# Linear attention with a gated feed-forward: other DRAM rows and transfers for the last 64 rows of x, for w1's last rows and for the folded output weight

## Chip, cores, metric

The kernel runs on one core of one Trainium2 chip. The metric is device microseconds of one execution; lower is better. Before the change three runs took 1108.54, 1109.60 and 1109.98 us (median 1109.6).

## What is computed

x is 2048 x 576, everything in fp32. Two branches read the normalized xn and are multiplied:

```
xn = layernorm(x)
q, k, v = heads(xn @ wqkv)                 # 32 heads of 18
phi(t) = (t + 1 if t > 0 else exp(t)) + 1e-6
kv = sum_s phi(k)_s v_s ;  z = sum_s phi(k)_s
s = concat_heads(phi(q) kv / (phi(q) z + 1e-6)) @ wo
g = silu(gelu(xn @ w1 + b1) @ w2 + b2)     # 4608 hidden units
out = x + s * g
```

## The kernel before, in words

**Precision.** TensorE multiplies in fp32r. Each operand is kept as a high part h (a cast) and a low part l (the rest), and a product is h·h + h·l + l·h: per 128 rows of the contraction three matmuls.

**The contraction of 576** is four blocks of 128 and a last block of 64 rows. These 64 rows ("the rest") are not three matmuls but one: their h and l rows are laid into the 128 partitions, and one matmul against a suitably doubled weight tile gives all terms.

**Stages.** (1) 0 to 157 us: normalize and transpose x, k and v projections, the state kv. (2) 157 to 291 us: the query projection (`query`, line 415), `fold_wo` (line 554), which multiplies kv into wo once so that attention needs one product per tile, and per token tile `transpose_p`, `attend`. (3) from 291 us: the feed-forward, in two halves of nine steps. A step takes four blocks of 128 hidden units: two `Up` objects n (line 963, 14 products in all, 7 matmuls of 512 columns each: six for two blocks of 128 rows, the seventh for the rest), then the down products (`pm`, line 1114). Both matrix products use a seven-product scheme (of Winograd's kind) over 2x2 blocks, so seven different sums of x's blocks are wanted, numbered 1 to 7. An `Up` takes them in the order 1, 6, 7, 5, 2, 3, 4. The first half has one set of x sums, the second half another; between them, in the ninth step, all x tiles are exchanged.

**x sums in DRAM.** `x_dram` holds the 28 blocks for the half that comes later; `X_PARTS` (line 1270) names the seven transfers of 1 MB each (h0, l0, s2, h1, l1, s1, s4), `X_AT` the step at which each is issued. The rests are made apart by the class `Rest` (line 775), for half 0 and half 1 beside stage 2: `gather` collects h and l of the 64 rows, `whole` adds them and sends them through `rr_dram` to shift partitions, `sums` forms the Winograd sums, `split` makes h and l again and stores them in `rq_dram`: two stores of 128 rows for each of two tiles. `load_rest` (line 822) reads one product's rest: two transfers, each of 32 DRAM rows read twice into 64 partitions, 2 KB a row: h into partitions 0 to 63, l into 64 to 127. Rests 1, 6 and 7 go beside their x parts into a free fifth block of h0, s2, h1; rests 5, 2, 3 and 4 into the tile `rxm` (`load_rests`, line 953: eight transfers).

**w1's last rows** lie in `we_dram`. `load_we` (line 678) reads for each n 64 rows of 3584 B, and the same rows again into the other 64 partitions: two transfers.

**fold_wo** computes kv·wo in groups of 126 rows, but the weight is wanted in blocks of 128 rows. The shift is done by DMA from SBUF to SBUF: of group i, the first k = 2i rows go to the end of block i-1 (line 581), the others, 126 - k, to the head of block i (line 584): transfers of 124, 122 and 120 rows. ScalarE (`split_kw`, line 261) casts a block as soon as it is there, then VectorE forms its low part (line 262).

**Order.** All DMAs here are issued by SP, one after the other. Up to the end of stage 2 and in the feed-forward the order of PE, DVE, ACT and POOL is the program's (`in_order`); SP's is chosen by the scheduler from the same program order. In the feed-forward `plans` (line 1322) names at which product a load, cast or sum is issued. DMAs take their completion semaphores from a ring of eight, so a DMA can only be issued when the one eight before it has landed.

Of the kernel before, what the change touches and what calls it, by code (L numbers as in the profile page):

```python
# [8 lines left out]
F32 = mybir.dt.float32  # L9
# [15 lines left out]
KT = 5  # L25
# [17 lines left out]
def linear_attention_gated_ffn(ctx, tc, x, wqkv, wo, w1, w1e, b1, w2, b2, out):  # L43
# [42 lines left out]
    def as2(ap):  # L86
        return ap.rearrange("p (a b) -> p a b", a=2)
# [26 lines left out]


    rr_dram = dram.tile([2, P, 512], F32, name="rr_dram")
    rq_dram = dram.tile([2, 2, P, 2, 512], F32, name="rq_dram")
    we_dram = dram.tile([WG, P, 2, WB * P], F32, name="we_dram")
    c_dram = dram.tile([2, P, QH, 2, HD], F32, name="c_dram")

# [433 lines left out]
    def fold_wo():  # L554

        (kr0, kw1), (kw2, kw3) = (
            (t[:, 0], t[:, 1]) for t in (kw_pair("kw01"), kw_pair("kw23"))
        )
        kw4 = stage(D, "kw4")
        kw = [kr0, kw1, kw2, kw3, kw4]  # L560

        for i, n, at in [(i, G, i * G) for i in range(4)] + [(4, 8, 4 * G), (4, P, 512)]:
            rows = GROUPS[i][1]
            for h in range(2):
                hs = slice(h * HD, (h + 1) * HD)
# [12 lines left out]
            if 0 < i and n < P:  # L578

                k = 2 * i  # L580
                nc.sync.dma_start(krs[-1][P - k :], kw[i][:k])
                if i < 4:
                    krs.append(stage(D, f"kr{i}"))
                    nc.sync.dma_start(krs[-1][: G - k], kw[i][k:G])
            elif i == 0:
                krs.append(kr0)

# [90 lines left out]
    def load_we(n):  # L678

        we_sb[n] = w1p.tile([P, WB, P], F32R, tag="we", name=f"we_{n}", bufs=2)  # L680
        dst = we_sb[n].bitcast(F32).rearrange("p b c -> p (b c)")
        g, q = divmod(n % NP, WG)
        src = we_dram[q, 32 * g : 32 * g + 32].rearrange("r v c -> (r v) c")
        for k in range(2):
            nc.sync.dma_start(dst[64 * k : 64 * k + 64], src)

    WE_AT = {1: 0, 2: 1, 3: 2, 5: 3, 7: 4, 6: 5, 4: 6}

# [83 lines left out]
    nc.gpsimd.memset(sgn[64:96, 1:2], 1.0)  # L772
    nc.gpsimd.memset(sgn[96:, 1:2], -1.0)

    class Rest:
        def __init__(self, half):
            self.half = half
# [1 line left out]

        def two(self, n):  # L780
            t = w1_tile("a", f"rest{self.half}{n}").rearrange("p k c -> p (k c)")
            return t[:, :512], t[:, 512:1024]

        def gather(self):
            self.q, lo = (v.bitcast(F32) for v in self.two("q"))
            for b in range(2):
                rows = slice(64 * b, 64 * b + 64)
                nc.sync.dma_start(self.q[rows], self.b[b][:64, 4].bitcast(F32))
                nc.sync.dma_start(lo[rows], self.b[b][64:, 4].bitcast(F32))
            self.lo = lo  # L790

        def whole(self):
            q, rr = self.q, rr_dram[self.half]
            nc.vector.tensor_tensor(q, q, self.lo, op=ADD)
            nc.sync.dma_start(rr, q)
            self.e, self.f = (v.bitcast(F32) for v in self.two("ef"))
            self.g, self.m = (v.bitcast(F32) for v in self.two("gm"))
            A0, B0, A1, B1 = (rr[32 * k : 32 * k + 32] for k in range(4))
            for k, (e, f) in enumerate(((A0, A1), (A1, B1)) * 2):
                nc.sync.dma_start(self.e[32 * k : 32 * k + 32], e)  # L800
                nc.sync.dma_start(self.f[32 * k : 32 * k + 32], f)
            nc.sync.dma_start(self.g[64:96], B0)
            nc.sync.dma_start(self.g[96:], A0)
            nc.sync.dma_start(self.m[64:96], B1)

        def split(self, k):
            src = (self.q, self.e)[k]
            h, l = t = self.two(f"s{k}")
            nc.scalar.copy(h, src)
            nc.vector.tensor_tensor(l, src, h.bitcast(F32), op=SUB)  # L810
            for v in range(2):
                nc.sync.dma_start(rq_dram[self.half, k, :, v], t[v].bitcast(F32))

        def sums(self):
            e, g, m, up = self.e, self.g, self.m, slice(64, P)
# [1 line left out]
            nc.vector.scalar_tensor_tensor(e[up], g[up], sgn[up, 1:2], e[up], op0=MUL, op1=ADD)  # L817
            nc.vector.tensor_tensor(e[64:96], e[64:96], m[64:96], op=SUB)

    REST_AT = {1: 0, 2: 1, 4: 3, 7: 4, 5: 5, 3: 6, 6: 7}  # L820

    def load_rest(half, i, dst):

        k, at = divmod(REST_AT[i], 4)
        for v in range(2):
            src = rq_dram[half, k, 32 * at : 32 * at + 32, v]
            nc.sync.dma_start(
                dst[64 * v : 64 * v + 64].bitcast(F32),
                bass.AP(tensor=src.tensor, offset=src.offset, ap=[[1024, 32], [0, 2], [1, 512]]),
            )  # L830

    EW1 = nc.gpsimd
    EL1 = nc.vector
# [22 lines left out]
    def beside(i, k):  # L856

        if k == 0:
            if i == 3:
                split_kw(3, nc.vector)  # L860
            if i == 4:
                xsum[0] = XSums(0, tmp_w1)
            if i == 5:
                xsum[1] = XSums(2, lambda name: as2(kw_pair(name).rearrange("p a d -> p (a d)")[:, :1024]))
            sums(i)
            if i in RESTS:
                half, what, *k = RESTS[i]
                if half not in rests:
                    rests[half] = Rest(half)
                getattr(rests[half], what)(*k)  # L870
        else:
            if i == 16:
                sums(i)
            if i == 17:
                z = xsum[1]
                z.split(z.u, z.s3, nc.vector)
            if i in SPLITS:
                half, n = SPLITS[i]
                z = xsum[half]
                if i in (8, 12):  # L880
                    z.place(not half)
                z.split(z.u if n == 3 else z.t, getattr(z, f"s{n}"), nc.vector)
                if not half:
                    spill(i - 8)
            if i == 12:
                w2_raw0.append(load_w2_raw(0))
                w1t[0] = W1(0)
            if i == 13:
                w1t[1] = W1(1)
            if i == 16:  # L890
                load_we(0)
                z = xsum[1]
                load_rest(1, 1, z.h0[:, 4])
                load_rest(1, 6, z.tiles[0][:, 4])
                load_rest(1, 7, z.h1[:, 4])
            if i == 17:
                w = w1t[0]
                w.hi("a"), w.lo("a")
                for j in (5, 6, 7, 4):
                    w.T(j)  # L900
                w.hi(6), w.lo(6)
            if i == 18:
                load_we(1)
                w = w1t[0]
                for j in ("c", "d"):
                    w.hi(j), w.lo(j)
# [44 lines left out]
    rxm = xp.tile([P, KT, 512], F32R, tag="xh1", name="rxm")  # L951

    def load_rests(half):
        out = {}
        for k, i in enumerate((5, 2, 3, 4)):
            out[i] = rxm[:, k]
            load_rest(half, i, out[i])
        return out

    mid = md.tile([P, 5, 512], F32, name="mid")  # L960
    m1_sb, u1_sb, u2_sb = (mid[:, i] for i in range(3))
# [297 lines left out]

    def x_operands(h0, l0, h1, l1, s1, s2, s4, rs):  # L1260
        A, B = slice(0, 2), slice(2, 4)
        rs = {1: h0[:, 4], 6: s2[:, 4], 7: h1[:, 4], **rs}
        return {i: (*v, rs[i]) for i, v in {
            1: (h0[:, A], l0[:, A]), 2: (h0[:, B], l0[:, B]), 4: (h1[:, B], l1[:, B]),
            7: (h1[:, A], l1[:, A]), 5: (s1[:, A], s1[:, B]), 6: (s2[:, A], s2[:, B]),
            3: (s4[:, A], s4[:, B]),
        }.items()}


    X_PARTS = {  # L1270
        "h0": (0, x_hi, 0, 1), "s4": (24, x_lo, 1, None), "l0": (4, x_lo, 2, None),
        "s2": (16, x_hi, 2, 6), "s1": (20, x_lo, 0, None), "h1": (8, x_hi, 3, 7),
        "l1": (12, x_lo, 3, None),
    }
    X_AT = {"h0": 8, "l0": 11, "s2": 11, "h1": 13, "l1": 13, "s1": 13, "s4": 14}
# [2 lines left out]
    def load_x_part(k):  # L1278
# [1 line left out]
        x_new[k] = make_tile(at, f"{k}r")  # L1280
        nc.sync.dma_start(x_new[k][:, :4].bitcast(F32), x_dram[:, a : a + 4])
        if i:
            load_rest(0, i, x_new[k][:, 4])

    UP = (1, 6, 7, 5, 2, 3, 4)
    NS = 28
# [49 lines left out]
    w2t[0].load_raw()  # L1336
    z = xsum[1]
    s2, s1, s4 = z.tiles
    xs = x_operands(z.h0, z.l0, z.h1, z.l1, s1, s2, s4, load_rests(1))
    seq = ExitStack()  # L1340
    seq.enter_context(in_order(nc.vector.engine, nc.scalar.engine, nc.gpsimd.engine, nc.tensor.engine))
    n_chunks = 2 * NC
    for step in range(n_chunks):
# [59 lines left out]
        if half == 1 and c >= 2:  # L1403
            for k in range(2 + 2 * plain):
                tiles = {}
                t, at, done = (6 + c, 0, 4) if k < 2 else (7 + c, 5, 9)
                def load(k=k, t=t, tiles=tiles):
                    tiles[0] = finish_tiles(k)
                    finish_load(t, k % 2, tiles[0])
# [74 lines left out]
```

## Time and profile before

| | us |
|---|---|
| median of three runs | 1109.6 |
| the profiled execution | 1109.0 |
| its span, first to last instruction | 1107.3 |
| outside the span | 1.7 |
| PE busy | 1094.5 |
| DVE busy | 799.7 |
| POOL busy | 454.2 |
| ACT busy | 453.1 |
| granted TensorE clock | 0.999 |

How to read it: an engine's busy time is what its instructions took; PE is TensorE. A row of the chain reads "start, length, what": the chain runs back from the last instruction through whatever released each one. A row of the timeline reads "start, length, engine, line, operation, out<-in", and in brackets how long the engine had been idle and who ended that. In the table by stretches the last two columns are the mean busy share of the 16 DMA engines and the rate at which they moved data. "SPq" is SP issuing a DMA. In names, `a`, `b`, `e`, `zy` are PSUM tiles of an `Up`; `h0r`, `s4r` and so on are the x parts read back for the second half; `wa`, `wc`, `wd` are w1 operands.

### The profile page before, as it was taken

Reading aid. Unit: us, or ns where it says so; the run is one execution under the profiler, and the core shown is the slowest. Engines: PE = TensorE matmul, PEld = TensorE weight load, DVE = VectorE, ACT = ScalarE, POOL = GpSimd, SP = SyncE. Lnnn points to the kernel's source line nnn. Section 1 sums busy time; section 2 is a strip of 40 time slices with the busy share of each in tenths; the row PEclk is TensorE's granted clock in tenths of the full one; section 3 lists DMA queues with packets and bytes.
Section 4 is the critical chain, followed back from the end, with each engine's and each line's share of the span. In section 5 each row is a group of like instructions: output and inputs, shape, how many; then the busy total and the mean of one; then the engine's idle time right before and its main releaser. Section 6 shows DMA issues by size and latency. Waiting matters only on the chain.

```text
span 1107.3 us, 18602 instructions
## 1 busy us (share of the span) xinstructions
PE 1094.5 (99%) x6972; PEld 1018.5 (92%) x6972; DVE 799.7 (72%) x1163; ACT 453.1 (41%) x768; POOL 454.2 (41%) x392
## 2 busy tenths in 40 slices
PE   8999999999999999999999999999999999999998
PEld 8999998999998998989989889799898998988977
DVE  7665447989687787978878878667485574664866
ACT  4554433343544354454443544524234243242342
POOL 4976424333353462453534633314234143242350
PEclk9999999999999999999999999999999999999999
DMA  8697842365879659576595689897877676777443
GB/s 329 254 372 255 290 172 62 135 241 174 267 266 328 207 203 326 188 280 246 188 341 180 236 290 342 295 338 253 266 232 212 216 230 212 237 224 222 138 141 150
DMA packets 85112, 264.03 MB, mean 238 GB/s; under 512 B 10397, under 2 KB 21149, under 8 KB 81439
## 3 DMA queue, kind: packets, MB, share of 16 engines
q1 hardware_dynamic: 85023, 262.85, 69.7%
q8 instruction: 55, 0.90, 0.3%
q14 instruction: 34, 0.28, 0.1%
HBM read 166.69 MB, written 94.18 MB: 236 GB/s over the span
## 4 chain that ended last, share of the span: by engine, by line
PE 93%; DMA 5%; DVE 1%; issue 0%; SPq 0%; POOL 0%; ACT 0%; DVEq 0%; ACTq 0%; POOLq 0%
PE pm L1114 32%; PE a L981 10%; PE e L981 10%; PE zy L981 10%; PE pv L237 5%; PE ps_s L642 5%; PE pk L237 5%; PE b L981 5%; PE pq L237 4%; PE pd L1234 2%; DMA s4r<-x_dram 1%; PE ps_kva L274 1%; DMA kr<-kw 1%; DMA s2r<-x_dram 1%; PE pt L208 1%; DMA h0r<-x_dram 1%
## 5 line engine op out<-in xcount | busy, mean ns | idle before, releaser
L1120 DVE TENSOR_TENSOR macc<-pm,macc 128x576 f32<-128x576 f32 x218 | 163.8, 752 | 54.6 <-PE pm L1114 53.7
L666 ACT CAST h_h<-g 128x512 fp32r<-128x512 f32 x204 | 120.9, 621 | 132.4 <-PE pm L1114 131.2
L669 DVE TENSOR_TENSOR h_l<-g,h_h 128x512 fp32r<-128x512 f32 x204 | 165.1, 816 | 0.0
L1080 POOL TENSOR_TENSOR mid<-g 128x512 f32<-128x512 f32 x34 | 43.9, 1291 | 147.7 <-ACT g L989 147.7
L1074 POOL TENSOR_TENSOR g<-g 128x512 f32<-128x512 f32 x34 | 55.1, 1621 | 58.0 <-DVE h_l L669 56.7
L989 ACT ACTIVATE g<-b,b1c 128x512 f32<-128x512 f32 x36 | 24.8, 688 | 117.4 <-DVE b L1007 117.4
L998 ACT COPY mid<-a 128x512 f32<-128x512 f32 x36 | 21.1, 587 | 118.7 <-PE a L981 118.7
L710 POOL TENSOR_TENSOR w1raw<-w1raw 128x256 f32<-128x256 f32 x18 | 16.9, 940 | 122.4 <-DVE wa L726 122.4
L1001 DVE TENSOR_TENSOR mid<-b,mid 128x512 f32<-128x512 f32 x36 | 24.7, 687 | 46.7 <-PE b L981 42.2
L1077 POOL TENSOR_TENSOR g<-g 128x512 f32<-128x512 f32 x34 | 55.2, 1624 | 2.7
L981 PE MATMUL a<-h0r,wa 128*128 128x512 f32 x144 | 50.5, 391 | 1.4 <-DMA wa<-op_a 1.4
L981 PE MATMUL a<-xh,wa 128*128 128x512 f32 x144 | 50.4, 390 | 0.0
L669 DVE TENSOR_TENSOR h_l<-mid,h_h 128x512 fp32r<-128x512 f32 x34 | 48.8, 1435 | 1.2
L1071 POOL TENSOR_TENSOR g<-g 128x512 f32<-128x512 f32 x34 | 46.7, 1373 | 2.7
L1007 DVE TENSOR_TENSOR b<-e,mid 128x512 f32<-128x512 f32 x36 | 25.2, 699 | 30.3 <-PE e L981 30.3
L1202 POOL TENSOR_TENSOR fin1l<-fin1h,fin1l 128x288 f32<-128x288 f32 x7 | 5.7, 808 | 100.4 <-DMA fin1l<-s_dram 72.1
L607 POOL TENSOR_TENSOR pbuf<-phiq,den 128x576 f32<-128x576 f32 x16 | 20.1, 1258 | 63.4 <-DVE den L606 44.6
L218 DVE TENSOR_TENSOR xl<-pt,xh 128x512 fp32r<-128x512 f32 (+1 forms) x17 | 11.2, 660 | 47.4 <-ACT xh L213 47.3
L1004 DVE TENSOR_TENSOR mid<-zy,mid 128x512 f32<-128x512 f32 x36 | 24.9, 691 | 24.2 <-PE zy L981 24.2
L306 POOL TENSOR_TENSOR w2r<-w2r 128x576 f32<-128x576 f32 x27 | 38.8, 1443 | 6.5 <-DMA w2r<-w 5.8
L1014 DVE TENSOR_TENSOR e<-e,mid 128x512 f32<-128x512 f32 x36 | 24.9, 691 | 19.8 <-PE e L981 19.8
L989 ACT ACTIVATE g<-e,b1c 128x512 f32<-128x512 f32 x36 | 24.8, 690 | 32.5 <-DVE e L1014 32.5
(811 smaller groups left out, 3606.6 us busy)
## 6 DMA issues: line engine op xcount, KB each, us to landing
we<-we_dram SPq DMA_DIRECT2D x72, 224.0 KB
op<-w2o SPq DMA_DIRECT2D x27, 576.0 KB
w2raw<-w SPq DMA_DIRECT2D x10, 1152.0 KB
w2r<-w SPq DMA_DIRECT2D x9, 1152.0 KB
w1raw<-w SPq DMA_DIRECT2D x18, 512.0 KB
op_a<-wa SPq DMA_DIRECT2D x18, 512.0 KB
op_c<-wc SPq DMA_DIRECT2D x18, 512.0 KB
op_d<-wd SPq DMA_DIRECT2D x18, 512.0 KB
```

The lines of the kernel that those rows point to most:

```text
L237: nc.tensor.matmul(ps[:, h, :HD], st, w[:, k, h * HD : (h + 1) * HD], start=(i == 0), stop=(i == len(seq) - 1),)
L642: nc.tensor.matmul(ps[:, h, :HD], st[:, k, :], w[:, k, h * HD : (h + 1) * HD], start=(i == 0), stop=(i == len(seq) - 1),)
L666: nc.scalar.copy(pair[0], src)
L669: eng.tensor_tensor(pair[1], src, pair[0].bitcast(F32), op=SUB)
L981: nc.tensor.matmul(ps, st, mv, start=first and n == 0, stop=n == len(seq) - 1, skip_group_check=True,)
L989: nc.scalar.activation(g, ps, AF.Gelu_apprx_tanh, bias=b1c[:, f : f + 1])
L1071: tt(src[5, pr], A(1, 0), A(1, 1), op=ADD)
L1074: tt(src[6, pr], src[5, pr], A(0, 0), op=SUB)
L1077: tt(src[3, pr], A(0, 1), src[6, pr], op=SUB)
L1080: tt(src[7, pr], A(0, 0), A(1, 0), op=SUB)
L1114: nc.tensor.matmul(ps[:, q, :HD], hs[p][st][:, cs], m[:, p, :], start=(n == 0 and i not in CHAIN), stop=(n == 5), skip_group_check=True,)
L1120: nc.vector.tensor_tensor(dst, src, dst, op=ADD)
```

## The change

* `rq_dram` is laid out by row and product instead of by tile: `[half, 32 rows, copy, h or l, 8 products, 512]`. `split` stores each product's 32 rows by themselves and twice (once per copy), h and l together: 6 stores for the first tile, 8 for the second, instead of 2 and 2.
* `load_rest` now reads 128 DRAM rows into 128 partitions; products that are neighbours in DRAM come in one transfer. Products 1, 7, 5 and 3 are neighbours and are read as one transfer of 128 rows of 8 KB into `rxm`; 2, 6 and 4 are read one by one (2 KB a row) into the fifth block of h0, s2 and h1. For that `gather` takes the rows in another order (six transfers instead of four).
* The rests of half 1 (the first to be used) are loaded in `beside` at i = 16.
* `load_we` reads both copies in one transfer of 128 rows.
* In `fold_wo` the transfers of 124, 122 and 120 rows become one of 112 rows and one of the other 12, 10 or 8.
* The multiply and add of two output tiles in the last step (`finish`) are planned four products later.

```diff
-    rq_dram = dram.tile([2, 2, P, 2, 512], F32, name="rq_dram")
+    rq_dram = dram.tile([2, 32, 2, 2, 8, 512], F32, name="rq_dram")
...
-                    nc.sync.dma_start(krs[-1][: G - k], kw[i][k:G])
+                    nc.sync.dma_start(krs[-1][:112], kw[i][k : k + 112])
+                    nc.sync.dma_start(krs[-1][112 : G - k], kw[i][k + 112 : G])
...
-        src = we_dram[q, 32 * g : 32 * g + 32].rearrange("r v c -> (r v) c")
-        for k in range(2):
-            nc.sync.dma_start(dst[64 * k : 64 * k + 64], src)
+        src = we_dram[q, 32 * g : 32 * g + 32]
+        row = WB * P
+        nc.sync.dma_start(
+            dst, bass.AP(tensor=src.tensor, offset=src.offset, ap=[[row, 64], [0, 2], [1, row]])
+        )
...
+    REST_AT = {2: 0, 4: 2, 1: 3, 7: 4, 5: 5, 3: 6, 6: 7}
...
-            for b in range(2):
-                rows = slice(64 * b, 64 * b + 64)
-                nc.sync.dma_start(self.q[rows], self.b[b][:64, 4].bitcast(F32))
-                nc.sync.dma_start(lo[rows], self.b[b][64:, 4].bitcast(F32))
+            for at, b, k, n in ((96, 0, 0, 32), (0, 0, 32, 32), (32, 1, 0, 64)):
+                for v, dst in ((0, self.q), (64, self.lo)):
+                    nc.sync.dma_start(
+                        dst[at : at + n], self.b[b][v + k : v + k + n, 4].bitcast(F32)
+                    )
...
-            for v in range(2):
-                nc.sync.dma_start(rq_dram[self.half, k, :, v], t[v].bitcast(F32))
+            for at in range(4):
+                if 4 * k + at in REST_AT.values():
+                    for v in range(2):
+                        nc.sync.dma_start(
+                            rq_dram[self.half, :, v, :, 4 * k + at],
+                            t[32 * at : 32 * at + 32].bitcast(F32),
+                        )
...
-    REST_AT = {1: 0, 2: 1, 4: 3, 7: 4, 5: 5, 3: 6, 6: 7}
-    def load_rest(half, i, dst):
-        k, at = divmod(REST_AT[i], 4)
-        for v in range(2):
-            src = rq_dram[half, k, 32 * at : 32 * at + 32, v]
-            nc.sync.dma_start(
-                dst[64 * v : 64 * v + 64].bitcast(F32),
-                bass.AP(tensor=src.tensor, offset=src.offset, ap=[[1024, 32], [0, 2], [1, 512]]),
-            )
+    def load_rest(half, at, n, dst):
+        rows = rq_dram[half].rearrange("r w v k c -> (r w v) (k c)")
+        nc.sync.dma_start(dst.bitcast(F32), rows[:, at * 512 : (at + n) * 512])
+    rx = []
+    def load_rests(half):
+        if not rx:
+            rx.append(xp.tile([P, KT, 512], F32R, tag="xh1", name="rxm"))
+        t = rx[0]
+        load_rest(half, REST_AT[1], 4, t[:, :4].rearrange("p k c -> p (k c)"))
+        return {i: t[:, REST_AT[i] - REST_AT[1]] for i in (1, 7, 5, 3)}
...
-                load_rest(1, 1, z.h0[:, 4])
-                load_rest(1, 6, z.tiles[0][:, 4])
-                load_rest(1, 7, z.h1[:, 4])
+                rests["x"] = load_rests(1)
+                for n, t in ((2, z.h0), (6, z.tiles[0]), (4, z.h1)):
+                    load_rest(1, REST_AT[n], 1, t[:, 4])
...
-    def load_rests(half):
-        out = {}
-        for k, i in enumerate((5, 2, 3, 4)):
-            out[i] = rxm[:, k]
-            load_rest(half, i, out[i])
-        return out
...
-        "h0": (0, x_hi, 0, 1), "s4": (24, x_lo, 1, None), "l0": (4, x_lo, 2, None),
-        "s2": (16, x_hi, 2, 6), "s1": (20, x_lo, 0, None), "h1": (8, x_hi, 3, 7),
+        "h0": (0, x_hi, 0, 2), "s4": (24, x_lo, 1, None), "l0": (4, x_lo, 2, None),
+        "s2": (16, x_hi, 2, 6), "s1": (20, x_lo, 0, None), "h1": (8, x_hi, 3, 4),
...
-                t, at, done = (6 + c, 0, 4) if k < 2 else (7 + c, 5, 9)
+                t, at, done = (6 + c, 0, 4) if k < 2 else (7 + c, 5, 13)
```

In the built program the changed kernel issues PE's, DVE's, ACT's and POOL's instructions in the same order as before; only which tile holds a rest differs. SP issues 29 DMAs fewer: 36 fewer for w1's last rows and 20 fewer loads of rests, 20 more stores of rests, 4 more in `gather` and 3 more in `fold_wo`.

More of the change, by code (lines that the diff above doesn't have):

```diff
@@ L781, in two @@
             t = w1_tile("a", f"rest{self.half}{n}").rearrange("p k c -> p (k c)")
-            return t[:, :512], t[:, 512:1024]
+            return t[:, :512], t[:, 512:1024], as2(t[:, :1024])
         def gather(self):
-            self.q, lo = (v.bitcast(F32) for v in self.two("q"))
-            for b in range(2):
-                rows = slice(64 * b, 64 * b + 64)
-                nc.sync.dma_start(self.q[rows], self.b[b][:64, 4].bitcast(F32))
-                nc.sync.dma_start(lo[rows], self.b[b][64:, 4].bitcast(F32))
-            self.lo = lo
+            self.q, self.lo, _ = (v.bitcast(F32) for v in self.two("q"))
+            for at, b, k, n in ((96, 0, 0, 32), (0, 0, 32, 32), (32, 1, 0, 64)):
[3 more added lines that the diff above has]
+                    )
         def whole(self):
@@ L795, in whole @@
             nc.sync.dma_start(rr, q)
-            self.e, self.f = (v.bitcast(F32) for v in self.two("ef"))
-            self.g, self.m = (v.bitcast(F32) for v in self.two("gm"))
-            A0, B0, A1, B1 = (rr[32 * k : 32 * k + 32] for k in range(4))
+            self.e, self.f, _ = (v.bitcast(F32) for v in self.two("ef"))
+            self.g, self.m, _ = (v.bitcast(F32) for v in self.two("gm"))
+            B0, A1, B1, A0 = (rr[32 * k : 32 * k + 32] for k in range(4))
             for k, (e, f) in enumerate(((A0, A1), (A1, B1)) * 2):
@@ L807, in split @@
             src = (self.q, self.e)[k]
-            h, l = t = self.two(f"s{k}")
+            h, l, t = self.two(f"s{k}")
             nc.scalar.copy(h, src)
             nc.vector.tensor_tensor(l, src, h.bitcast(F32), op=SUB)
-            for v in range(2):
-                nc.sync.dma_start(rq_dram[self.half, k, :, v], t[v].bitcast(F32))
+            for at in range(4):
[5 more added lines that the diff above has]
+                        )
         def sums(self):
@@ L948, in linear_attention_gated_ffn @@
     BIAS = {2: 0, 7: 1, 3: 1, 4: 0}
-    rxm = xp.tile([P, KT, 512], F32R, tag="xh1", name="rxm")
-    def load_rests(half):
-        out = {}
-        for k, i in enumerate((5, 2, 3, 4)):
-            out[i] = rxm[:, k]
-            load_rest(half, i, out[i])
-        return out
     mid = md.tile([P, 5, 512], F32, name="mid")
@@ L1261, in x_operands @@
         A, B = slice(0, 2), slice(2, 4)
-        rs = {1: h0[:, 4], 6: s2[:, 4], 7: h1[:, 4], **rs}
+        rs = {2: h0[:, 4], 6: s2[:, 4], 4: h1[:, 4], **rs}
         return {i: (*v, rs[i]) for i, v in {
@@ L1282, in load_x_part @@
         if i:
-            load_rest(0, i, x_new[k][:, 4])
+            load_rest(0, REST_AT[i], 1, x_new[k][:, 4])
     UP = (1, 6, 7, 5, 2, 3, 4)
@@ L1338, in linear_attention_gated_ffn @@
     s2, s1, s4 = z.tiles
-    xs = x_operands(z.h0, z.l0, z.h1, z.l1, s1, s2, s4, load_rests(1))
+    xs = x_operands(z.h0, z.l0, z.h1, z.l1, s1, s2, s4, rests["x"])
     seq = ExitStack()
```

## The prediction

> **What bounds the kernel now.** I read the page's busy times first, then PE's waits, then the chain around the two waits that the change can reach, then SP's issues there.
>
> ```profile
> PE 1094.5 (99%) x6972; PEld 1018.5 (92%) x6972; DVE 799.7 (72%) x1163; ACT 453.1 (41%) x768; POOL 454.2 (41%) x392
> PE 93%; DMA 5%; DVE 1%; issue 0%; SPq 0%; POOL 0%; ACT 0%; DVEq 0%; ACTq 0%; POOLq 0%
> ```
>
> TensorE is the bound, and the change leaves its matmuls alone. So only idle time of PE can be won, 1107.3 - 1094.5 = 12.8 us, part of it the head and the tail. Which part is within reach, the table of PE's waits tells (total us, times, longest):
>
> ```profile
> PE warm L267 <- POOL ident masks.py:199: 1.6, 1, 1.6
> PE e L981 <- DVE b L1007: 1.5, 1, 1.5
> PE a L981 <- DMA wa<-op_a: 1.4, 1, 1.4
> PE pk L237 <- DVE wk_l L262: 0.7, 1, 0.7
> PE ptp L624 <- DVE phiq L247: 0.6, 1, 0.6
> ...
> PE ps_s L642 <- DVE th L630: 0.2, 1, 0.2
> ```
>
> Two belong to edited code: `wa<-op_a` (the exchange of the x tiles between the halves) and `ptp`, `ps_s` (beside `fold_wo`). The others lie in the head or in the last step, whose instruction order the change leaves alone; the later planning of `finish` moves nothing there, since no POOL instruction stands between the old place and the new. In front of the product `a` only one DMA ever kept PE waiting, so the 72 transfers of w1's rests made none of it wait: halving their number saves SP time that nobody waits for, and counts as nothing in every step but the exchange.
>
> **Part 1: the shifts in fold_wo.** The rows are SP's issues, ACT's casts and PE's two gaps, then two regular passages for comparison.
>
> ```profile
> 167.73 1.00 SPq L584 DMA_DIRECT2D kr<-kw  x1
> 168.83 0.88 SPq L581 DMA_DIRECT2D kr<-kw  x1
> 180.05 0.67 ACT L261 CAST kw_h<-kr 128x576 fp32r<-128x576 f32 x1 [4.46 <-DMA kr<-kw]
> 180.63 0.65 ACT L244 ACTIVATE eq<-pq 128x576 f32<-128x576 f32 x1
> 182.90 0.74 PE L624 MATMUL ptp<-ident,pbuf 128*128 128x128 f32 x5 [0.62 <-DVE phiq L247]
> 183.80 0.50 PE L642 MATMUL ps_s<-kw_h,th 128*128 128x288 f32 x2 [0.17 <-DVE th L630]
> ...
> 168.83 11.14 DMA kr<-kw
> ...
> 279.44 0.55 PE ptp L624 x5
> ```
>
> A transfer of 122 rows issued at 167.73, with six rows behind it at 168.83, lands 11.14 us later. ACT sits idle for it for 4.46 us, so the next activation `eq`, VectorE's `phiq` and with them the PSUM tile that `ptp` needs are late: PE idles 0.62 + 0.17 = 0.79 us. With the refill of its pipeline it is more: from `ptp` to `ps_s` 183.80 - 182.90 = 0.90 us pass instead of 0.55. So the gain lies between 0.8 us (gaps alone) and 0.79 + 0.35 = 1.1; I take 1.1.
>
> It needs the block before ACT comes to it, about 4.5 us before 180.05. The trace has no 112-row shift. The nearest regular row, 128 rows of 2 KB through `rr_dram` (below), lands in 2.05 us. Three more issues of up to 1.0 us each put the last part of this block at about 171 us, its landing at about 173: cover of some 2.5 us. If that cover is gone, the gain is nothing.
>
> ```profile
> 191.96 0.36 SPq L795 DMA_DIRECT2D rr_dram<-wa_rest0q  x1
> 194.01 0.32 SPq L800 DMA_DIRECT2D wa_rest0ef<-rr_dram  x1
> ```
>
> The Trainium skill (DMA: Bandwidth & Descriptors, "Why a DMA increments its semaphore by 16 and not by 1") gives a reason: a transfer uses as many of the 16 engines as divide its outer dimension, so 4 engines for 124 rows, 2 for 122, 16 for 112. The trace agrees, with 11.14 us against 2.05; by that rule the new transfers land like the regular one, and the sum stays.
>
> **Part 2: the exchange between the halves.** Chain, SP's issues, PE:
>
> ```profile
> 681.07 16.35 DMA s4r<-x_dram
> 699.27 6.23 DMA wa<-op_a
> ...
> 662.74 0.32 SPq L1281 DMA_DIRECT2D h0r<-x_dram  x1
> 663.11 1.18 SPq L827 DMA_DIRECT2D h0r<-rq_dram  x2
> 664.33 0.60 SPq L685 DMA_DIRECT2D we<-we_dram  x1
> ...
> 668.12 0.43 SPq L1281 DMA_DIRECT2D l0r<-x_dram  x1
> 671.19 0.32 SPq L1281 DMA_DIRECT2D s2r<-x_dram  x1
> ...
> 677.57 0.33 SPq L1281 DMA_DIRECT2D s1r<-x_dram  x1
> ...
> 681.77 16.17 SPq L827 DMA_DIRECT2D rxm<-rq_dram  x8
> ...
> 699.27 0.58 SPq L750 DMA_DIRECT2D wa<-op_a  x1
> ...
> 694.28 0.39 PE L981 MATMUL a<-h0r,we 128*128 128x512 f32 x1
> 703.82 0.39 PE L981 MATMUL zy<-rxm,we 128*128 128x512 f32 x1
> 705.63 0.47 PE L981 MATMUL a<-h0r,wa 128*128 128x512 f32 x1 [1.43 <-DMA wa<-op_a]
> ```
>
> SP may have eight DMAs under way: s1r, the eighth behind l0r, goes out when l0r has landed, and the eight pieces of `rxm` take 16.17 us, until s4r has landed at 681.07 + 16.35 = 697.42. Only then come two DMAs for w1's rest and `wa`, at 699.27. It lands too late by 1.43 us; counted from the matmul before, 705.63 - 703.82 - 0.23 (one matmul's step, 1.59 us a product by seven) = 1.6 us.
>
> *Removed.* With one transfer for `rxm`, `wa` is the eighth behind s2's rest. That lands right after s2r, which s4r's issue at 681.07 shows landed. So `wa` goes out near 682, some 17 us earlier, and its 0.5 MB, behind 1 MB of `rxm` and 0.45 MB, are there long before 704. **Gain 1.6 us.**
>
> *Added.* The first product of the new half needs its rest at 694.28. Before, that lay beside h0r, loaded first; now it lies in `rxm`, issued last. Does it land in time? Everything from h0r to `rxm` is one queue of data. Its size by the page's KB: seven parts of 1024, three rests of 256, 512 each for `wd` and the two small w1 blocks, 1024 for `rxm`, and ahead of it w1's rest of 448 and a store of 512: some 10.9 MB (of 1024 KB), 11.2 million bytes. The rates:
>
> ```profile
> 662.00:672.00 10.00, 10.00 (x51) 8.52 (x50) 7.39 (x10) 4.71 (x9) 5.24 (x4) 1.00 0.99 293
> 672.00:682.00 10.00, 10.00 (x77) 10.00 (x76) 9.12 (x13) 4.56 (x8) 5.84 (x4) 1.00 1.03 369
> 682.00:690.00 8.00, 8.00 (x62) 8.00 (x62) 6.67 (x11) 4.21 (x5) 0.00 (x0) 1.00 1.03 361
> ...
> 686.00:690.00 4.00, 4.00 (x32) 4.00 (x32) 2.92 (x6) 3.07 (x3) 0.00 (x0) 1.00 1.01 414
> 692.00:694.00 2.00, 2.00 (x13) 1.82 (x13) 1.88 (x4) 0.00 (x0) 1.68 (x1) 1.00 1.06 221
> 694.00:697.40 3.40, 3.40 (x16) 2.79 (x16) 3.40 (x4) 2.69 (x3) 2.24 (x2) 1.00 0.37 107
> ```
>
> The last two columns are the DMA engines' busy share and GB/s. Where 1 MB parts of 128 rows flow, 414 GB/s; where the 64-row pieces of `rxm` flow, 221 at the same full share. *Early bound:* all at 414 GB/s: 11.2 / 0.414 = 27 us from 662.7, and 2 us to land: 691.8. Nothing waits. *Late bound:* the rates as they were: 2.9 + 3.7 + 2.9 MB by 690, the other 1.7 in 4 us: 694; and a few engines trail, for after 694 the share falls to 0.37 and s4r still needs until 697.4: 3.4 us more. `rxm` at 698, a new wait of 3.7 us. Between them: the 64-row transfers ahead (three rests, half of w1's rest, 1.0 million bytes) become 128-row ones: 4.6 us at 221 GB/s become 2.5 at 414. That takes 2.1 us off 694, and of the trailing I keep 2.5 us, as the stretch at half rate, in which it grew, is gone: 694.4 to 694.7. **New wait 0.4 us** (0 to 3.7).
>
> The Trainium skill (SBUF — State Buffer, "Door 1: The DMA port swizzle") has partitions 0 to 63 reach only 8 of the 16 DMA ports of SBUF, so half rate; the trace agrees, 221 against 414 GB/s. By that rule the early bound is the nearer one; if the port were not the cause, it would be the late one.
>
> **Part 3: what lies beside other work.** Each half's rests cost SP ten more stores and two more gathers, at 0.3 to 0.7 us an issue some 6 us in 60 us of attention; no wait of PE is there between 184 and 704. Half 1's rests, `rxm` with them, are now read when the old kernel read three of them, at 277.42; 1 MB at 414 GB/s with 2 us to land is there by 283, and PE needs it 1.4 us after 291.10. Cover 9 us; gone, it would cost what it is late.
>
> ```profile
> 277.42 1.24 SPq L827 DMA_DIRECT2D xh<-rq_dram  x2
> ...
> 291.10 1.59 PE a L981 x7
> ```
>
> **Sum.** 1109.0 (the profiled execution: span 1107.3 and 1.7 around it) - 1.1 - 1.6 + 0.4 = **1106.7 us**. The median of the runs, 1109.6, lies 0.6 higher; the difference of -2.3 us is what is forecast. A measurement of this kernel can tell about 0.2%, 2.2 us, from no change: the forecast lies just beyond it, and 1109.0 - 2.7 = 1106.3 is the most that can be won.
>
> **The rivals.**
> 1. *The wait moves instead of going.* The first product now needs what SP issues last; if the engines trail as before, `rxm` is 1 to 3.7 us late and 1109.0 - 2.7 + 1 to 3.7 gives 1107.3 to 1110.0, say 1108.5. For it: s4r landing at 697.42, 3 us after the new need. Against: the half-rate stretches ahead are gone.
> 2. *Slower: rests read out of DRAM at half rate.* The new `rq_dram` has rows 16 KB apart of which 2 or 8 KB are read. If that layout, like the old one 4 KB apart, is what gave 221 GB/s, then the rests' 0.8 and `rxm`'s 1.05 million bytes take 8.4 us instead of 4.5, and `rxm` comes at 694.6 + 3.9 = 698.5 at best, at 702 with the late bound: 4.2 to 7.7 us of wait, and 1109.0 - 2.7 + 4.2 to 7.7 = 1110.5 to 1114.0, say 1112. It decides from a landing after 694.3 + 2.7 = 697.0 on. Against: w1's rest, read from rows that lie without gaps, was as slow (245 GB/s), and shares the 64 partitions with the rests.
>
> ```profile
> 700.00:702.00 2.00, 2.00 (x10) 1.66 (x9) 0.18 (x1) 1.90 (x3) 0.00 (x0) 1.00 1.06 245
> ```
>
> [...]
>
> 3. *The shift stays late* (the row count was not the reason): 1109.0 - 1.6 + 0.4 = 1107.8.
>
> **How the numbers follow.** Forecast with a wait of 0 to 0.8 us, 1106.3 to 1107.1: 0.50, most of it beyond 0.2% (0.42). Rival 1: 0.27, within 0.2%. Rival 3: 0.06, within. Rival 2: 0.17, beyond 0.2% slower but for 0.02. So faster 0.42, same 0.43, slower 0.15. The range takes in rival 1 and the lower part of rival 2: 1106.0 to 1111.0.
>
> **What would show it.** Right: no wait of ACT for `kr` over 1 us, `ptp` without a gap; no wait for `wa`; a wait of `a<-rxm` under 1 us; 64-row stretches at 221 GB/s gone from the exchange. Wrong: a long wait for `rxm` (rivals 1, 2; by the rate of its own stretch one tells them apart), `kr` still landing near 180, or a new wait near 291.

## The result, and the profile after

The changed kernel takes **1106.1 us** (median of 16 runs, 1105.4 to 1108.2), against 1108.9 for the kernel before on the same chips (1107.8 to 1112.5). The ratio is 0.9975, with an interval of 0.9968 to 0.9983: 2.8 us faster, 0.25%. The profiled execution took 1106.0 us with a span of 1104.3.

The waits of TensorE in the changed kernel, all of them (total us, times, longest):

```profile
PE e L984 <- DVE b L1010: 1.6, 1, 1.6
PE warm L267 <- POOL ident masks.py:199: 1.6, 1, 1.6
PE pk L237 <- DVE wk_l L262: 0.6, 1, 0.6
PE pk L237 <- DVE xh L217: 0.6, 1, 0.6
PE pt L208 <- DVE xn L187: 0.5, 1, 0.5
```

The three that the change could reach, `ptp`, `ps_s` and `a` for `wa`, are gone, and none has come in their place: no row names `rxm`. The other five stood there before.

Beside `fold_wo`, ScalarE's cast and TensorE's two passages in the timeline:

```profile
175.05 0.68 ACT L261 CAST kw_h<-kr 128x576 fp32r<-128x576 f32 x1
...
182.06 0.71 PE L625 MATMUL ptp<-ident,pbuf 128*128 128x128 f32 x5
182.62 0.50 PE L643 MATMUL ps_s<-kw_h,th 128*128 128x288 f32 x2
```

ScalarE makes three casts out of `kr`. This is the second, which started at 180.05 before the change, after a wait of 4.46 us. Now it starts at 175.05 and no bracket stands behind it: the block lay there when ScalarE came to it. From `ptp` to `ps_s` pass 0.56 us, as in a regular passage, and `ps_s` starts at 182.62 instead of 183.80: 1.18 us earlier.

The exchange, SP's issues and then TensorE's first product of the new half:

```profile
672.54 0.32 SPq L1284 DMA_DIRECT2D s4r<-x_dram  x1
675.04 0.32 SPq L833 DMA_DIRECT2D rxm<-rq_dram  x1
677.54 0.53 SPq L686 DMA_DIRECT2D we<-we_dram  x1
678.20 0.51 SPq L753 DMA_DIRECT2D wa<-op_a  x1
...
692.90 0.40 PE L984 MATMUL a<-h0r,wa 128*128 128x512 f32 x1
693.14 0.39 PE L984 MATMUL a<-rxm,we 128*128 128x512 f32 x1
```

`wa` goes out 21 us earlier than before (678.20 for 699.27), and the matmul on `rxm` follows its neighbour by 0.24 us, without a gap. When `rxm` landed can be read from SP, which waits for it with the next store:

```profile
SPq L1194 <- DMA rxm<-rq_dram: 1.6, 1, 1.6
```

SP had nothing to issue from 689.77 on, so `rxm` was there at about 691.4, 1.8 us before the matmul that needs it. The table by stretches for the same time (the last three columns: granted clock, busy share of the DMA engines, GB/s):

```profile
662.00:672.00 10.00, 10.00 (x55) 8.72 (x54) 8.14 (x11) 4.41 (x7) 4.69 (x4) 1.00 0.96 356
672.00:682.00 10.00, 10.00 (x77) 10.00 (x76) 9.18 (x12) 4.20 (x8) 5.32 (x4) 1.00 1.01 415
682.00:690.00 8.00, 8.00 (x62) 8.00 (x61) 6.17 (x10) 4.02 (x5) 0.00 (x0) 1.00 1.01 415
...
692.00:694.00 2.00, 2.00 (x10) 1.65 (x9) 1.97 (x3) 0.44 (x1) 2.00 (x2) 1.00 1.03 413
```

The engines are as full as before, but in the last three rows, where they moved 369, 361 and 221 GB/s, they now move 413 to 415.

### The profile page after: what moved, and what is told of

Read it like the earlier page. It is cut to its first block, busy times and chain, and to the rows that moved or that the text cites. A ratio compares the mean times of both kernels' runs of the same rounds, so it can differ in the third digit from the quotient of the medians.

```text
span 1104.3 us, 18544 instructions
## 1 busy us (share of the span) xinstructions
PE 1094.0 (99%) x6972; PEld 1018.5 (92%) x6972; DVE 799.6 (72%) x1163; ACT 453.0 (41%) x768; POOL 454.5 (41%) x392
## 4 chain that ended last, share of the span: by engine, by line
PE 98%; DVE 1%; issue 0%; POOL 0%; ACT 0%; DVEq 0%; ACTq 0%; POOLq 0%
PE pm L1117 34%; PE a L984 10%; PE e L984 10%; PE zy L984 10%; PE pv L237 5%; PE ps_s L643 5%; PE pq L237 5%; PE b L984 5%; PE pk L237 5%; PE pd L1237 2%; PE ps_kva L274 1%; PE pt L208 1%; PE ptp L625 1%; PE ps_kw L567 1%; PE warm L267 0%
```

## The experiments

Ratios are to the kernel before, run on the same chip in the same series. "us over the changed kernel" compares medians; the changed kernel's are 1106.14 and, in the last series, 1106.08.

### 1. The fold alone, undone and done

`fold_old` is the changed kernel with the old shifts, `b_fold` the kernel before with the new ones.

```diff
-                    nc.sync.dma_start(krs[-1][:112], kw[i][k : k + 112])
-                    nc.sync.dma_start(krs[-1][112 : G - k], kw[i][k + 112 : G])
+                    nc.sync.dma_start(krs[-1][: G - k], kw[i][k:G])
```

> The changed kernel with the shifts of fold_wo as before (124, 122 and 120 rows in one transfer each). Theory: the fold's part of the gain, 1.1 us, goes back: the kr block of 122 rows lands near 179 to 180 again, ScalarE idles over 3 us for it, TensorE shows two gaps of together some 0.8 us at ptp and ps_s near 182, and nothing else differs. Ratio to the kernel before 0.9985 (changed kernel: 0.9975). Rival, the fold is hidden behind other work and the exchange gave everything: ratio 0.9975.

> The kernel before, with only the shifts of fold_wo in 112 rows and the rest. Theory: no wait of ScalarE for kr over 1 us, no gap at ptp and ps_s, 0.8 to 1.1 us won; the wait for wa near 704 stays as it is: ratio 0.9990. Rival (the two parts of the change are not independent, the exchange shifts with it): ratio 0.9980 or 1.000.

Measured: `fold_old` 1107.0 us, ratio 0.9988 (0.9979 to 0.9997); `b_fold` 1107.2, ratio 0.9988 (0.9977 to 0.9998). In `fold_old` the late block and TensorE's two gaps are back:

```profile
181.18 0.67 ACT L261 CAST kw_h<-kr 128x576 fp32r<-128x576 f32 x1 [4.16 <-DMA kr<-kw]
...
184.08 0.74 PE L624 MATMUL ptp<-ident,pbuf 128*128 128x128 f32 x5 [0.42 <-DVE phiq L247]
184.98 0.52 PE L642 MATMUL ps_s<-kw_h,th 128*128 128x288 f32 x2 [0.17 <-DVE th L630]
```

Undone, the fold costs 0.9 us over the changed kernel (medians of two series); done alone it wins 1.3. The forecast 1.1 lies between, and each interval holds it, but each is some 1 us wide to either side. One half of `b_fold`'s expectation did not show: its profiled execution has no wait for `wa`, which went out at 694.56 there; why so early is open. The wait for `wa` differs from run to run, as do the times of the kernel before (4.7 us from lowest to highest in its 16 runs, against 2.8 for the changed one).

### 2. Fewer rows, or a row count that divides?

`fold_halves` cuts each shift into two equal transfers, 62, 61 or 60 rows, in place of 112 and the rest.

```diff
-                    nc.sync.dma_start(krs[-1][:112], kw[i][k : k + 112])
-                    nc.sync.dma_start(krs[-1][112 : G - k], kw[i][k + 112 : G])
+                    m = (G - k) // 2
+                    nc.sync.dma_start(krs[-1][:m], kw[i][k : k + m])
+                    nc.sync.dma_start(krs[-1][m : G - k], kw[i][k + m : G])
```

> The changed kernel with each shift cut into two equal transfers, 62+62, 61+61 and 60+60 rows, in place of 112 and the rest. As many transfers as in the changed kernel. Theory (the row count decides how many DMA engines share a transfer; 61 has no divisor up to 16 but 1): 61 rows by one engine are as late as 122 by two, 11 us, so ScalarE waits for kr until 179 or later and 1.1 us is lost: ratio 0.9985 or a little above. Rival (a shorter transfer is simply done earlier): the halves land within 3 to 6 us, no wait, ratio 0.9975.

Measured: 1116.46 us, ratio 1.0071 (1.0057 to 1.0085): not 1.1 but 10.3 us over the changed kernel. The chain, ScalarE's wait, TensorE's wait:

```profile
168.19 19.06 DMA kr<-kw x2
...
187.36 0.67 ACT L261 CAST kw_h<-kr 128x576 fp32r<-128x576 f32 x1 [9.54 <-DMA kr<-kw]
...
190.20 1.30 PE L626 MATMUL ptp<-ident,pbuf 128*128 128x128 f32 x5 [6.64 <-DVE phiq L247]
```

The block is complete only at 187, 18 us after its first half was issued (169.01); the chain runs through two transfers. Half as many rows are slower, so it is not the length of a transfer that made it late; the rival falls. The size was missed: the expectation took the halves to land side by side, 11 us after their issue. ScalarE's waits go with the row count in the first block too: 2.43 us for 124 rows (kernel before), 4.14 for 62 and 62, none for 112 and 12. The table by stretches shows a second cost (the last three columns: granted clock, busy share of the 16 DMA engines, GB/s):

```profile
184.00:186.00 2.00, 0.00 (x0) 0.00 (x0) 0.00 (x0) 0.00 (x0) 0.00 (x0) 1.00 0.06 24
186.00:188.00 2.00, 0.00 (x0) 0.00 (x0) 0.00 (x0) 0.64 (x2) 0.00 (x0) 0.66 0.07 25
188.00:190.00 2.00, 0.00 (x0) 0.00 (x0) 1.84 (x4) 2.00 (x6) 0.00 (x0) 0.50 0.64 144
190.00:192.00 2.00, 1.80 (x8) 1.83 (x9) 1.96 (x4) 0.90 (x2) 1.41 (x1) 0.50 0.09 19
192.00:194.00 2.00, 2.00 (x12) 2.00 (x12) 1.83 (x6) 0.22 (x1) 0.32 (x1) 0.64 0.04 8
```

TensorE stood idle, its clock fell to 0.5, and for 3 us after the wait it still worked at 0.5 to 0.64. The first row also shows how few engines carry the late block: a busy share of 0.06 at 24 GB/s is that of one engine in 16 (0.0625). In the kernel before, the last 2 us ahead of its late block (178 to 180) had 0.13 and 45 GB/s, that of two.

### 3. Half the partitions, or twice the number of transfers?

Both of these cut every read of a rest and of w1's last rows in two, out of the new layout: `all_64` by partitions (64 each, as before the change), `all_cols` by columns (128 partitions, half a row). The edits in `load_rest`, `all_64` first; `load_we` likewise:

```diff
-        nc.sync.dma_start(dst.bitcast(F32), rows[:, at * 512 : (at + n) * 512])
+        for p in range(n):
+            for j in range(2):
+                nc.sync.dma_start(
+                    dst[64 * j : 64 * j + 64, p * 512 : (p + 1) * 512].bitcast(F32),
+                    rows[64 * j : 64 * j + 64, (at + p) * 512 : (at + p + 1) * 512],
+                )
```
```diff
-        nc.sync.dma_start(dst.bitcast(F32), rows[:, at * 512 : (at + n) * 512])
+        for p in range(2 * n):
+            nc.sync.dma_start(
+                dst[:, p * 256 : (p + 1) * 256].bitcast(F32),
+                rows[:, at * 512 + p * 256 : at * 512 + (p + 1) * 256],
+            )
```

> The changed kernel with all reads of the rests and of w1's last rows in 64 partitions a transfer, one product each, as many and as large as before the change; the layout in DRAM stays the new one. Theory (half rate into 64 partitions, and 8 DMAs under way at most): the exchange goes as before the change, 220 to 250 GB/s where such transfers flow, s4r lands near 696, wa goes out near 698 and TensorE waits 1.2 to 1.6 us for it near 703: ratio 0.9989. Rival (the layout in DRAM was what slowed the reads): they run at about 400 GB/s, no wait, ratio 0.9975.

> The changed kernel with each of these reads cut into two by columns instead: all 128 partitions, half the bytes of a row (1 KB for a rest, 1792 B for w1's last rows), the same number of transfers as in all_64. Theory (the rate matters, not the number): about 380 to 410 GB/s through the exchange, s4r lands near 690, wa goes out near 692 and is there by 698; no wait of TensorE, ratio 0.9975. Rival (the number of transfers holds SP up, whatever their rate): wa goes out after 697 as in the kernel before, wait 1.0 to 1.6 us, ratio 0.9985 to 0.9989.

Measured: `all_cols` 1106.19 us, ratio 0.9983 (0.9974 to 0.9991), as the changed kernel and with no wait for `wa` or `rxm`. `all_64` 1111.62, ratio 1.0028 (1.0013 to 1.0043): **slower than the kernel before**, with runs from 1107.1 to 1116.0. The stretches from 672 on, `all_64` first, then `all_cols`:

```profile
672.00:682.00 10.00, 10.00 (x77) 10.00 (x76) 9.12 (x13) 4.07 (x8) 5.45 (x4) 1.00 1.03 346
682.00:690.00 8.00, 8.00 (x62) 8.00 (x61) 6.30 (x10) 4.15 (x5) 0.00 (x0) 1.00 1.01 380
690.00:694.00 4.00, 3.43 (x22) 2.81 (x20) 3.41 (x5) 0.00 (x0) 2.70 (x2) 1.00 0.89 192
```
```profile
672.00:682.00 10.00, 10.00 (x77) 10.00 (x76) 9.12 (x13) 4.01 (x7) 5.74 (x4) 1.00 1.02 413
682.00:690.00 8.00, 8.00 (x62) 8.00 (x61) 6.58 (x10) 4.22 (x5) 0.00 (x0) 1.00 0.99 381
690.00:694.00 4.00, 4.00 (x26) 3.66 (x25) 3.12 (x4) 0.02 (x1) 2.40 (x2) 1.00 0.76 230
```

The same number of transfers of the same bytes: in the first rows 346 GB/s at a share of 1.03 by partitions, 413 by columns. In the second both move 380 to 381, and in the third `all_cols` does not fill its engines (0.76), so the reading rests on the first; experiments 4 and 6 bear it out. Neither the number of transfers nor the layout in DRAM is what cost the rate; the partition span is. What was late in `all_64` is not `wa`, as expected, but what the reordered kernel needs first:

```profile
694.35 0.50 PE L991 MATMUL a<-rxm,we 128*128 128x512 f32 x1 [0.92 <-DMA rxm<-rq_dram]
```

> The same file as all_64, for a second profile: the first one had 0.9 us of wait for rxm and 1107.4 us, while the median of its runs was 1111.6. Theory (half rate makes rxm late by an amount that differs from run to run, and a wait of about 3 us or more halves the granted clock for some 4 us as well): a wait of 2 to 4 us in front of a<-rxm, then a stretch of 4 us at a clock of 0.5 to 0.6, 1110 to 1114 us. Rival (the median of all_64 comes from some other place): wait below 1 us again with a time over 1110.

The second profile of `all_64` took 1106.9 us with 0.44 us of wait for `rxm`. Neither theory's numbers came: both profiles caught executions near the short end of its range, and where the longest lost up to 9 us was not seen in a trace. The mean granted clock of each run of `all_64` is known, though: 0.999 and 1.000 in the two shortest, 0.994 to 0.997 in the six of 1111.7 us and more. So the long ones did have stretches at a lower clock, as the theory says; that a late `rxm` caused them is not shown.

### 4. One transfer, half the partitions

`rest_halves` keeps the four products in one row, but cuts each read in two by partitions.

```diff
-        nc.sync.dma_start(dst.bitcast(F32), rows[:, at * 512 : (at + n) * 512])
+        for j in range(2):
+            nc.sync.dma_start(
+                dst[64 * j : 64 * j + 64].bitcast(F32),
+                rows[64 * j : 64 * j + 64, at * 512 : (at + n) * 512],
+            )
```

> The changed kernel with each read of rests and of w1's last rows cut into two by partitions, 64 each, the columns whole: rxm in two transfers of 64 rows of 8 KB. Few transfers, half rate. Theory: wa no longer waits behind rxm's pieces and goes out near 684 to 686, so no wait for wa; but rxm, issued last and needed first, lands at 694 to 698 and TensorE waits for it in front of a<-rxm, 0.5 to 3.7 us, say 2: ratio 0.9993. Rival (with 8 KB rows 64 partitions are no slower): rxm lands near 691, no wait, ratio 0.9975.

Measured: 1115.28 us, ratio 1.0056 (1.0042 to 1.007), 9.1 us over the changed kernel. TensorE's wait, and the stretches around it:

```profile
702.45 0.77 PE L990 MATMUL a<-rxm,we 128*128 128x512 f32 x1 [8.00 <-issue]
...
694.00:700.00 6.00, 0.45 (x2) 0.01 (x1) 2.82 (x2) 0.00 (x0) 2.21 (x2) 0.72 1.01 217
...
698.00:702.00 4.00, 0.00 (x0) 0.00 (x0) 0.00 (x0) 0.00 (x0) 0.00 (x0) 0.50 1.01 222
702.00:706.00 4.00, 3.55 (x9) 2.84 (x9) 0.00 (x0) 2.70 (x3) 0.00 (x0) 0.50 1.02 351
```

The profile names no releaser for the 8 us ("issue"), but the matmul behind them is the first that reads `rxm`, and until 702 the engines were full at 217 to 222 GB/s. With rows of 8 KB, too, 64 partitions get half the rate. SP's order was near the expected one: `wa` went out at 688.02 (expected 684 to 686) and no wait names it. The price was double the upper bound of 3.7 us, and after it came 4 us at half the clock. The profiled execution is the longest of the six (1112.6 to 1117.4), so its wait is no typical one.

### 5. The kernel before, with `wa` ahead of the rests

`b_wa_early` plans the loads of w1 for the second pair two products earlier in the exchange step of the kernel before.

```diff
-            add(base + (16 if change else 14), load_we, 2 * step + 3)
+            add(base + 14, load_we, 2 * step + 3)
...
-            add(base + (16 if change else 14), make, W1Loaded, w1t, 2 * step + 3)
+            add(base + 14, make, W1Loaded, w1t, 2 * step + 3)
```

> The kernel before, with one thing moved: the loads of w1 for the second product pair after the exchange (its last rows, wa, wc, wd) are planned two products earlier, so SP issues them ahead of s4r and of rxm's eight pieces. All transfers as before. Theory (wa is late only because its issue stands behind eight pieces, which wait for s4r's landing): wa lands before 700, its wait of 1.4 us goes, 1.6 us won: ratio 0.9986. Rival (the DMA engines at half rate are full and something must be late): s4r or rxm's last pieces are late instead by 1 to 3 us; ratio 0.9995 to 1.001.

Measured: 1114.24 us, ratio 1.0054 (1.0034 to 1.0074). The theory (a place in SP's queue is all that `wa` lacks) falls. The rival's wait holds: with `wa` out at 681.30 its wait is gone, and the last pieces of `rxm` are late instead. The rival's ratio, at most 1.001, was too low: it counted the wait and not the lower clock behind it (third column from the right, 0.57).

```profile
702.51 0.77 PE L981 MATMUL e<-rxm,we 128*128 128x512 f32 x1 [2.74 <-DMA rxm<-rq_dram]
...
702.00:706.00 4.00, 3.49 (x9) 2.81 (x10) 0.70 (x1) 0.69 (x1) 0.00 (x0) 0.57 0.69 195
```

With the old reads something was late in both orders; the order chose what.

### 6. The partition span alone

`b_128` is the kernel before with only this: each rest in one transfer into 128 partitions out of the old layout, and w1's last rows likewise.

```diff
-            for v in range(2):
-                src = rq_dram[half, k, 32 * at : 32 * at + 32, v]
-                nc.sync.dma_start(
-                    dst[64 * v : 64 * v + 64].bitcast(F32),
-                    bass.AP(tensor=src.tensor, offset=src.offset, ap=[[1024, 32], [0, 2], [1, 512]]),
-                )
+        src = rq_dram[half, k, 32 * at : 32 * at + 32, 0]
+        nc.sync.dma_start(
+            dst.bitcast(F32),
+            bass.AP(tensor=src.tensor, offset=src.offset, ap=[[512, 64], [0, 2], [1, 512]]),
+        )
```

> The kernel before, with only the partition span of two reads changed: each rest comes by one transfer into 128 partitions, out of the old layout in DRAM (each 2 KB row read twice), and so do w1's last rows. No second copy in DRAM, no four products in one transfer, the rest of product 1 still beside h0, the shifts of fold_wo as before. (High and low parts of the last 64 rows are paired otherwise than they should be, so those products come out with other values; no instruction takes longer or shorter for it.) Theory (the 128 partitions are what counts): about 400 GB/s through the exchange, wa out near 684 and no wait for it, 1.6 us won, the fold's 1.1 us not: ratio 0.9985. Rival (the new layout, or one transfer in place of four, is what counts): wa still waits over 1 us, ratio 0.9995 to 1.0.

Measured: 1106.99 us, ratio 0.9987 (0.9977 to 0.9996), 1.55 us below the kernel before. SP's issues and two stretches:

```profile
676.60 6.25 SPq L828 DMA_DIRECT2D rxm<-rq_dram  x4
682.94 0.56 SPq L685 DMA_DIRECT2D we<-we_dram  x1
685.43 0.33 SPq L752 DMA_DIRECT2D wa<-op_a  x1
...
672.00:682.00 10.00, 10.00 (x77) 9.99 (x76) 9.23 (x13) 4.75 (x9) 5.83 (x4) 1.00 1.01 400
682.00:690.00 8.00, 8.00 (x62) 8.00 (x61) 7.04 (x11) 4.01 (x6) 0.00 (x0) 1.00 1.00 409
```

By the median the whole gain of the exchange is there without a second copy in DRAM and without four products in one transfer. Whether a right pairing of high and low parts can be read out of the old layout at this rate was not tried. `b_fold` and `b_128` together win 1.3 + 1.55 = 2.9 us, the whole change 2.8: the two parts add up, as far as intervals of some 1 us to either side can tell.

### 7. A version that beats both

With the change in place one wait of the steady part is left, 1.6 us in the last step: VectorE makes two low parts before it forms `b`. In the changed kernel:

```profile
1067.29 0.76 DVE L670 TENSOR_TENSOR w__11489<-w2raw,w__11489 128x576 fp32r<-128x576 f32 x1
1067.98 1.28 DVE L670 TENSOR_TENSOR hp_l<-g,hp_h 128x512 fp32r<-128x512 f32 x1
1069.18 0.69 DVE L1010 TENSOR_TENSOR b<-e,mid 128x512 f32<-128x512 f32 x1
```

`dve_later` makes them after it; the edit moves nothing else.

```diff
-                add(base + (2, 3, 8, 9)[f], w2t[step].lo, ("p", f))
+                add(base + (2, 3, 8, 10)[f], w2t[step].lo, ("p", f))
...
-                (0, 0, 7, 8), (0, 1, 8, 9), (1, 0, 10, 10), (1, 1, 10, 11), (0, 2, 11, 12),
+                (0, 0, 7, 8), (0, 1, 8, 10), (1, 0, 10, 10), (1, 1, 10, 11), (0, 2, 11, 12),
```

> The changed kernel, with two VectorE instructions of the last step (the low parts of one w2 block and of one h tile) planned after the product that TensorE waits on there, instead of ahead of it. Theory: VectorE forms b 2 us earlier, the 1.58 us wait of TensorE in front of e near 1068 goes, and the moved instructions are needed only some 6 us later: 1.4 to 1.7 us won, ratio 0.9960. Rival (VectorE is the bound of that stretch, so the wait comes back at the next product or at pd): ratio 0.9970 to 0.9975.

> The changed kernel as it is, for comparison with dve_again on one chip: ratio 0.9975, one wait of 1.6 us in front of e near 1068.

> The same file as dve_later, on one chip with the changed kernel: 1.4 to 1.6 us below it, ratio 0.9961; if it is within 0.5 us of the changed kernel, the wait at 1068 was covered by something later.

Measured: `dve_later` 1105.25 us, ratio 0.9965 (0.9950 to 0.9979). On one chip: `after_again` 1106.08 (ratio 0.9979, 0.9970 to 0.9988) and `dve_again` **1104.46** (ratio 0.9969, 0.9958 to 0.9981), 1.62 us less. VectorE in `dve_again`:

```profile
1067.50 0.70 DVE L1010 TENSOR_TENSOR b<-e,mid 128x512 f32<-128x512 f32 x1
1068.11 0.75 DVE L670 TENSOR_TENSOR w__11489<-w2raw,w__11489 128x576 fp32r<-128x576 f32 x1
1068.78 1.30 DVE L670 TENSOR_TENSOR hp_l<-g,hp_h 128x512 fp32r<-128x512 f32 x1
```

`b` comes before the two, and behind the first 20 us the list of waits names none of TensorE any more. The ratios alone do not exclude the rival (0.9970 lies in both intervals); the comparison on one chip does: all six runs of `dve_again` (1104.2 to 1105.7) lie below all eleven of `after_again` (1105.9 to 1107.7).

## Why the prediction was right, point by point

* **What can be won** (2.3 us forecast, at most 2.7): right in the main. The medians differ by 2.75 us, 0.4 more than forecast, because the new wait did not come; the profiled executions differ by 3.0, a little more than the bound. Of the 3.0, 1.18 come from the fold and 1.6 from `wa`. The small remainder, which the prediction did not have and no run explains, is the last store: from the end of VectorE's last instruction to the end of the span pass 3.1 us (1104.3 - 1101.23) instead of 3.4 (1107.3 - 1103.94). Before, then after:

```profile
1103.58 0.36 DVE L1184 TENSOR_TENSOR xs<-xs 128x192 f32<-128x192 f32 x1
```
```profile
1100.87 0.36 DVE L1187 TENSOR_TENSOR xs<-xs 128x192 f32<-128x192 f32 x1
```

* **Part 1, 1.1 us:** right in place and size (experiment 1), and so is the cover, since no wait of ScalarE for `kr` is left. The reason given stood against its own rival: 61 rows were slower than 122 (experiment 2). The Trainium skill (DMA: Bandwidth & Descriptors, "Why a DMA increments its semaphore by 16 and not by 1") has a transfer use as many engines as divide its outer dimension, and always the lowest-numbered ones; 61 rows would then sit on one engine, and both halves on the same one. The traces agree: a busy share of 0.06 for 61 rows and 0.13 for 122, and 18 us for the two halves.
* **Part 2, removed, 1.6 us:** right; `wa` went out even 4 us earlier than worked out. One thing was not seen: the wait of the kernel before is not a fixed 1.6 us. A profile of `b_fold` is without it. On that chip the shortest run of the kernel before (1107.30) lies 1.45 us above the shortest of the changed one (1105.85), little more than the fold alone. That the 1.6 of one profiled execution is also the gain by the medians (`b_128`: 1.55, with an interval of 0.4 to 2.5) is in part luck.
* **Part 2, added, 0.4 us:** wrong by its whole size, in the harmless direction. The early bound came true: 691.8 worked out, about 691.4 measured. The 2.5 us kept for trailing engines were the failed term: with 128-row transfers throughout, the engines moved 395 to 415 GB/s from 672 to 694, at a busy share of 1.00 to 1.03. Still, `rxm` came only 1.8 us before it was needed.
* **The cause of the half rate:** right, and now shown. Same layout, same number, same bytes: 346 GB/s by 64 partitions, 413 by 128 (experiment 3); the new layout by 64 partitions in few transfers: 217 to 222 (experiment 4); old layout with 128 partitions: 400 to 409 (experiment 6). Rival 2, the layout in DRAM, falls. The Trainium skill (SBUF — State Buffer, "Door 1: The DMA port swizzle") gives about 218 GB/s as the limit of 8 ports; the 217 to 222 measured in experiment 4 agree within 2%.
* **Rivals 1 and 2, their price:** too low. A late `rxm` was priced by the wait alone, up to 7.7 us over a kernel without it. Where it was late, a profiled execution with 8.0 us of wait took 11.3 us longer (1117.35 against 1106.03; the medians differ by 9.1). Some 2.2 of the other 3.3 us are the halved clock, 4.4 us of work at 0.5 behind the wait; 0.9 are longer waits in the first 20 us, which have nothing to do with it. Since `rxm` was in time, neither rival came; but the bet was larger than the text said, because the new order puts what is needed first at the end of the queue. With the old reads it loses 3.1 us to the kernel before (`all_64`).
* **Part 3:** right; no wait near 291, and none in the stage that writes the rests.

## What to carry to other kernels

Where the DMA engines are full, look at the bytes that they move, not at their busy share: here a share of 1.0 at half the rate meant transfers that span half the partitions, and another order only chose which tile was late. Let each transfer span all 128 partitions with a row count that 16 divides, even at the price of storing rows twice, and cut a ragged one into a part of that kind and a rest. Before moving what is needed first to the end of a queue, work out what a late arrival costs, the slow clock behind it included.

## What the runs showed of the hardware that was not expected

* **A wait of 2.7 us was enough to halve the clock.** Behind 6.6 us (experiment 2), 8.0 us (4) and 2.74 us (5) of idle TensorE the granted clock was at 0.5 for the next 3.1 to 4.4 us of work; behind 1.43 us in the kernel before and 0.92 in `all_64` it stayed at 1.00. By the clock records of the traces it fell 3.1, 2.2 and 2.4 us after the idle time began and stayed at 0.5 for 6.8, 10.2 and 3.4 us, which are twice, three times and once 3.41 us. The Trainium skill (TensorE: Matmul & The Clock Gate, "Why this matters for your kernels") warns of gaps of more than about 3 us; here 2.74 were enough.
* **Kernels with half-rate transfers scattered more, with one exception.** The runs of one kernel in one series lay within 2.8 us (changed), 3.0 (`all_cols`) and 2.5 (`b_128`), but within 4.6 to 5.4 (before), 4.7 (`rest_halves`), 7.4 (`b_wa_early`) and 8.9 (`all_64`). The exception is `b_fold`, with the old reads and 3.0.
* **VectorE at about half speed beside GpSimd, but not always.** In the last step the same subtraction of 128x512 takes 1.30 us where it overlaps GpSimd's work (at 1068.78, shown in experiment 7), and 0.68 two microseconds after GpSimd has ended. GpSimd's last two instructions there and VectorE's later one, in `dve_again`:

```profile
1067.43 0.81 POOL L1205 TENSOR_TENSOR fin<-fin 128x288 f32<-128x288 f32 x1
1068.31 1.21 POOL L1206 TENSOR_TENSOR fin<-fin 128x288 f32<-128x288 f32 x1
```
```profile
1071.81 0.68 DVE L670 TENSOR_TENSOR hp_l<-g,hp_h 128x512 fp32r<-128x512 f32 x1
```

Yet the subtraction at 1068.11 (128x576, experiment 7) overlaps GpSimd's work too and takes 0.75 us, as elsewhere in the kernel where it is not slowed. That the two contend is an inference from these times; no run took one of them away, and when they do is open.
